# Batch 2's attention numerators in one run, batch 3's k and kv earlier, and PSUM banks placed by hand between batches 0 and 1

## The chip, the cores and the metric

The kernel runs on one core of a Trainium2 chip. The metric is the device time in microseconds (us) of one execution, as the median of several. A profile is one further execution, taken with the hardware profiler; its span runs from the first to the last instruction of the program, and its own device time is a little longer than its span. Engines are named as the profile names them: PE is TensorE's matmuls and PEld its weight loads, DVE is VectorE, ACT is ScalarE, POOL is GpSimd and SP is SyncE, which only issues DMAs here. L533 is line 533 of the kernel before.

## The reference, cut to what matters

Linear attention with the feature map phi, then a token-and-channel mixer, for 8 batches of 8 heads, 576 tokens and 64 columns a head (512 columns in all). All arrays are float32.

```python
phi = lambda x: np.where(x > 0, x, np.exp(x) - 1.0) + 1.0
kv  = einsum('bhsd,bhse->bhde', phi(k), v)
z   = sum(phi(k), axis=2)
num = einsum('bhsd,bhde->bhse', phi(q), kv)
den = einsum('bhsd,bhd->bhs', phi(q), z)[..., None] + 1e-06
x   = (num / den)  # batch, tokens 576, columns 512
h   = relu(x.T @ w_tok1) @ w_tok2          # 576 -> 256 -> 576, along the tokens
u   = x + h.T
out = u + relu(u @ w_ch1) @ w_ch2          # 512 -> 1536 -> 512, along the columns
```

## The kernel before, in words

All matmuls are in bf16 with float32 sums in PSUM, which the kernel holds as one tile of eight banks (128 partitions x 512 float32 each). The 576 tokens of a batch are four slabs of 128 rows (R = 4) and a tail of 64; the tails of two batches share one slab of 128.

For each batch n the steps are, with the names of the code:

- `phi` (L166): exp on ScalarE (`phi_exp`, L148, tile e), x+1 and max on VectorE (`phi_add`, L154, tile y), their minimum on VectorE (`phi_end`, L162, tiles kp and qp). Each is done in two halves c = 0, 1. `prep_k` (L725) is phi of k and the cast of v (`vcast`, L173, tile vs); `k_exp` is only the two exps of a later batch's k.
- `kv` (L181): 72 small matmuls (L188) give kv and z of all heads in two banks; two ScalarE copies (L194) put them into `kvbd`. The first 36 need the first halves of kp and vs, the others the second.
- phi(q) is transposed into qT, by TensorE for batches 0 and 1, by two DMA transposes (`qtr_dma`, L218) from batch 2 on.
- `nd`: numerator and denominator, and the quotient x. In batches 1 and 2 it is six separate steps nd00 to nd21 (L282), each with two or four matmuls of 128 x 130 (L229), and three VectorE instructions (L238, L240, L241). From batch 3 on it is `nd_all` (L249): 40 matmuls of 64 rows x 65 columns (L258) into banks 2 to 7, in three rounds, and eleven VectorE instructions (L267, L269, L271, L278).
- `mm1` (L296): 10 matmuls, two relus on ScalarE (L305, tile ar). `mm2` (L307): ar times w_tok2, and u = x + h.T on VectorE (L327). Batch 1 does this in halves of the columns (`mm2_half`, L342): its first two slabs get x by an identity matmul (L351) and are copied out by ScalarE (L357), its last two by a VectorE addition (L359); `mm2(1, [R])` is batch 1's tail (L315, L323).
- u is transposed to uT: by TensorE in batch 1 (`utr`, L362, transposes L370, evicted by DVE L374 and ACT L376) and for the first tail (`utr_tail`, L508), by DMA transposes (`utr_dma`, L517) from batch 2 on.
- `mm3` (L527): 12 groups (mc) of four matmuls of 512 columns (L533), a relu each (ACT L540, or DVE L537 where dve is set) into cr. `mm3_tail` (L542) does the same for a pair's tails, four mc to a bank.
- `mm4` (L553): 12 accumulating matmuls (L559) to an output slab t, then `mm4_end`: DVE adds u (L576, L586) and GpSimd issues the output's DMA. From batch 3 on the output is made of fewer, other products (L695); their sums of weights are `weight_sums` (L609) on GpSimd.

The order is written out by hand. `run(bigs, fill)` (L877) walks a list of big steps (an mm3 group, an mm3 tail, or four matmuls of mm4) and after big step s it issues all fill steps with the number s. Each engine takes its instructions in the order of the program, and so do the DMA queues of SP and GpSimd. Batch 0's block (L897) ends with twelve steps `m4_0(kc)`, each a matmul for four output slabs; after the last come mm4_end, mm2_half, utr and mm2 of batch 1 (L913). Batch 1's block (L924) has 30 big steps: 12 mm3 groups, three tails, and slabs 4 to 8 of mm4 in three steps each; the numbers in `at1` and the lists under it place batch 2's and batch 3's steps in it.

`bank()` and `banks()` (L65, L70) without a number hand out banks 0 to 3 singly and banks 4 to 7 in pairs, in a ring: a step that is handed a bank waits until its last reader is done. With a number they give that bank. Up to batch 1's block most steps take the ring; from batch 2 on the banks are written out.

Of the kernel before, what the change touches and what calls it, by code (L numbers as in the profile page):

```python
# [18 lines left out]
def kernel(  # L19
# [26 lines left out]
    R = 4  # L46
# [98 lines left out]
    def phi_exp(nm, n, j0, nj):  # L145
        f = raw[nm, rb(n)][:, j0:j0 + nj].rearrange("p j f -> p (j f)")
        e = work.tile([128, 2 * TD], BF16, name="e", tag="e", bufs=4)[:, :nj * TD]
        nc.scalar.activation(out=e, in_=f, func=AF.Exp)  # L148
        live["e", j0] = e
# [8 lines left out]
    def phi_end(nm, n, j0, nj):  # L158
        c, i = divmod(j0, 2)
        dst = (kp if nm == "k" else qp)[:, c, :, i:i + nj]  # L160
        e, y = live["e", j0], live["y", j0][:, :nj * TD]
        live["phi"] = nc.vector.tensor_tensor(  # L162
            out=dst.transpose([0, 2, 1, 3]), in0=e.rearrange("p (i t d) -> p i t d", i=nj, t=T),
            in1=y.rearrange("p (i t d) -> p i t d", i=nj, t=T), op=ALU.min)
# [16 lines left out]
    def kv(n, cs):  # L181
        b = n % 2
        ps = banks(4 if n > 2 else None)[:, :, 0:2 * D1].rearrange(
# [112 lines left out]
    def mm1(n):  # L296
        b = n % 2
        ps = banks(4 if n > 2 else None)
# [8 lines left out]
    def mm2(n, rs, add=False):  # L307
# [4 lines left out]
            None if n < 3 else 4 if rs[0] else 6)  # L312
# [29 lines left out]
    def mm2_half(n, c):  # L342
        b = n % 2
        cs = COLS[c]
        for rs in ([0, 1], [2, 3]):
            ps = banks()[:, 0].rearrange(
# [15 lines left out]
    def utr(n, js):  # L362
        b = n % 2
        for jp in js:
            tp = two16()[:, 0].rearrange(
                "p (j r) c -> p j r c", j=2)
# [5 lines left out]
            dst = uT[b][:, :, 2 * jp:2 * jp + 2].transpose([0, 2, 1, 3])  # L372
            if jp == 0:
                nc.vector.tensor_copy(out=dst, in_=tp)  # L374
            else:
                nc.scalar.copy(out=dst, in_=tp)  # L376

# [147 lines left out]
    def mm3(n, mc, kjs=range(NDM), dve=False):  # L527
        b = n % 2
        if kjs[0] == 0:
            part_of[mc] = bank((0, 1, 0, 1, 2, 3, 0, 1, 2, 3, 0, 1)[mc] if n > 1 else None)  # L530
# [11 lines left out]
    def mm3_tail(i, late=True):  # L542
        ps = bank((2, 3, 0)[i] if late else None).rearrange("p (m s) -> p m s", m=4)
# [9 lines left out]
    def mm4(p, t, kcs, wait=False):  # L553
        if kcs[0] == 0:
            held[t] = bank({0: 2, 1: 3, 2: 0, 3: 2, 8: 3 if p == B // 2 - 1 else 2}[t] if p else None)
# [300 lines left out]
    def steps(n):  # L856

        out_ = [("kv", lambda: kv(n, range(2)))] if n < 3 else []
# [3 lines left out]
        for i, rs in enumerate(([0, 1], [2, 3], [4])) if n < 3 else ():  # L862
            for g in range(2):
                out_.append((f"nd{i}{g}", lambda g=g, rs=rs: nd(n, g, rs)))
        if n > 2:
            out_.append(("nd", lambda: nd_all(n)))
# [21 lines left out]
    m3t_0 = [lambda i=i: mm3_tail(i, False) for i in range(3)]  # L888
# [4 lines left out]
    def m4_0(kc):  # L893
        for t in range(R):
            mm4(0, t, [kc], wait=True)
# [16 lines left out]
    for nm, fn in first[1:2] + late + first[2:3] + first[0:1] + first[3:]:  # L912
# [3 lines left out]
        lambda: mm4_end(0, 2), lambda: mm2_half(1, 1), lambda: utr(1, [0]),  # L916
# [16 lines left out]
    fill += [(27, lambda: weight_sums(0, 2)), (28, lambda: kv(3, range(2)))]
    fill += [(29, lambda: k_exp(4))]
# [92 lines left out]
```

## Time and profile before

| | |
|---|---|
| median of three runs | 256.38 us (256.32 to 256.69) |
| the profiled execution, its own time | 256.18 us |
| its span | 254.3 us |
| batch 0's block and the change to batch 1, up to the first mm3 of batch 1 | to 52.62 us |
| batch 1's block, up to the first mm3 of batch 2 | 52.62 to 86.61 us |
| batches 2 to 7 | 86.61 to 254.3 us |
| DMA engines busy, queues of SP and GpSimd | 46.2% and 22.4% of the span |

The page gives busy times and their share of the span, the granted clock of TensorE in 40 slices, and the chain of work that ended last. A timeline gives instructions of one engine in order of time, merged by line, with the engine's idle time before them and what ended it. The start of a DMA and its landing come from the trace's issues. Instructions of one engine overlap a little: a row's length is the time from start to result, and the next may start before it is over.

### The profile page before, as it was taken

How to read it: one execution, taken by the hardware profiler on the slowest of the kernel's cores; microseconds unless marked ns; L12 is line 12 of the kernel's file. 1: busy time of each engine (PE TensorE's matmuls, PEld its weight loads, DVE VectorE, ACT ScalarE, POOL GpSimd, SP SyncE). 2: the span in 40 equal slices, each digit the busy share in tenths (PEclk: the TensorE clock that was granted, in tenths of full speed). 3: DMA queues.
4: the chain of work that ended last, by engine and by line, in shares of the span. 5: the costliest groups of instructions: out<-in, count | busy, mean ns of one | idle time of the engine just before them, and what ended most of it. 6: DMA issues, size and time to landing. Idle time of an engine off the chain costs nothing.

```text
span 254.3 us, 5671 instructions
## 1 busy us (share of the span) xinstructions
PE 246.2 (97%) x2338; PEld 145.8 (57%) x2338; DVE 162.3 (64%) x288; ACT 138.0 (54%) x217; POOL 68.2 (27%) x84
## 2 busy tenths in 40 slices
PE   7999999989999999999999999999999999999993
PEld 3574455544744444444488545675588545764863
DVE  5965768856767495537955398948864353933543
ACT  4765781559673469515957168565863165127400
POOL 9670120110001763991002600051003500150000
PEclk9999999999999999999999999999999999999999
DMA  6999999999819976459855966669272440445034
GB/s 251 258 203 265 366 233 363 279 261 389 316 42 175 289 261 216 96 131 333 327 125 115 372 148 214 133 176 335 86 116 44 100 110 0 82 61 127 3 92 114
DMA packets 49769, 48.37 MB, mean 190 GB/s; under 512 B 30096, under 2 KB 35600, under 8 KB 49744
## 3 DMA queue, kind: packets, MB, share of 16 engines
q1 hardware_dynamic: 41568, 34.87, 46.2%
q0 software_dynamic: 7632, 12.49, 22.4%
q10 hardware_dynamic: 544, 0.66, 1.1%
q8 instruction: 18, 0.29, 0.5%
q14 instruction: 7, 0.06, 0.1%
HBM read 35.85 MB, written 9.44 MB: 178 GB/s over the span
## 4 chain that ended last, share of the span: by engine, by line
PE 80%; DMA 8%; ACT 4%; POOL 3%; DVE 2%; issue 1%; SPq 0%; POOLq 0%; ACTq 0%; DVEq 0%
PE ps L533 28%; PE ps L695 15%; PE ps L559 14%; PE ps L302 6%; PE ps L547 4%; DMA k_raw<-in_k_dram 4%; PE ps L315 4%; DMA wc<-in_moe_w_ch_dram 4%; PE ps L648 4%; PE ps L188 2%; ACT e L148 2%; PE ps L258 1%; DVE obuf L576 1%; ACT cr L540 1%; PE ps L229 1%
## 5 line engine op out<-in xcount | busy, mean ns | idle before, releaser
L533 PE MATMUL ps<-uT,wc 128*128 128x512 bf16 x384 | 87.2, 379 | 0.8 <-DVE obuf L576 0.4
L540 ACT ACTIVATE cr<-ps 128x512 bf16<-128x512 f32 x91 | 53.1, 600 | 38.9 <-PE ps L533 38.5
L533 PEld LDWEIGHTS <-wc 128*128 128x128 bf16 x384 | 36.9, 98 | 44.3 <-issue 2.2
L559 PE MATMUL ps<-wc,cr 128*128 128x512 bf16 x144 | 34.5, 379 | 0.1
L708 POOL TENSOR_TENSOR obuf<-obuf,q_raw 128x512 f32<-128x512 f32 x4 | 5.1, 1267 | 77.3 <-ACT w L700 58.8
L327 DVE TENSOR_TENSOR u<-ps,x 128x1024 bf16<-128x1024 f32 x12 | 14.7, 1224 | 12.7 <-PE ps L315 12.6
L559 PEld LDWEIGHTS <-cr 128*128 128x128 bf16 x144 | 13.5, 98 | 14.8 <-issue 0.6
L148 ACT ACTIVATE e<-q_raw 128x1152 bf16<-128x1152 f32 x16 | 18.0, 1159 | 7.1 <-DMA q_raw<-in_q_dram 7.1
L630 DVE TENSOR_TENSOR v_raw<-cr 128x768 bf16<-128x768 bf16 (+1 forms) x15 | 10.3, 688 | 15.7 <-ACT cr L540 15.7
L581 POOL DMA_DIRECT2D out_dram<-obuf x12 | 7.3, 613 | 48.1 <-DVE obuf L576 48.1
L148 ACT ACTIVATE e<-k_raw 128x1152 bf16<-128x1152 f32 x16 | 18.2, 1162 | 3.7 <-DMA k_raw<-in_k_dram 3.6
L706 DVE TENSOR_TENSOR obuf<-ps,u 128x512 f32<-128x512 f32 x16 | 11.0, 690 | 12.4 <-PE ps L695 9.5
L695 PE MATMUL ps<-k_raw,v_raw 128*128 128x256 bf16 x144 | 16.7, 273 | 0.0
L695 PEld LDWEIGHTS <-cr 128*128 128x128 bf16 x144 | 14.0, 98 | 2.9
L695 PEld LDWEIGHTS <-v_raw 128*128 128x128 bf16 x144 | 13.9, 98 | 2.8 <-issue 0.8
L271 DVE TENSOR_TENSOR x<-ps,dens 128x768 bf16<-128x768 f32 x15 | 14.4, 958 | 0.5
L194 ACT CAST kvbd<-ps 64x260 bf16<-64x260 f32 x14 | 5.2, 373 | 17.1 <-PE ps L188 17.0
L302 PE MATMUL ps<-x,w 128*128 128x512 bf16 x56 | 14.4, 379 | 0.0
L162 DVE TENSOR_TENSOR kp<-e,y 128x1152 bf16<-128x1152 bf16 x16 | 11.7, 753 | 3.7 <-ACT e L148 3.4
L173 ACT CAST vs<-v_raw 128x1152 bf16<-128x1152 f32 x12 | 13.5, 1161 | 0.0
L154 DVE TENSOR_SCALAR y<-k_raw 128x1152 bf16<-128x1152 f32 x16 | 11.7, 752 | 2.5 <-DMA k_raw<-in_k_dram 2.5
L162 DVE TENSOR_TENSOR qp<-e,y 128x1152 bf16<-128x1152 bf16 x16 | 12.1, 758 | 1.6 <-ACT e L148 0.3
(132 smaller groups left out, 362.8 us busy)
## 6 DMA issues: line engine op xcount, KB each, us to landing
k_raw<-in_k_dram SPq DMA_DIRECT2D x16, 576.0 KB, 7.1
q_raw<-in_q_dram SPq DMA_DIRECT2D x16, 576.0 KB, 6.3
v_raw<-in_v_dram SPq DMA_DIRECT2D x14, 576.0 KB, 10.0
out_dram<-obuf POOLq DMA_DIRECT2D x8, 512.0 KB, 6.7
wc<-in_moe_w_ch_dram POOLq DMA_DIRECT2D x8, 384.0 KB, 10.1
out_dram<-obuf POOLq DMA_DIRECT2D x12, 256.0 KB, 7.3
out_dram<-obuf POOLq DMA_DIRECT2D x6, 128.0 KB, 5.5
cr<-in_v_dram POOLq DMA_DIRECT2D x2, 288.0 KB, 7.5
```

What stands on the lines that cost most here:

```text
L148: nc.scalar.activation(out=e, in_=f, func=AF.Exp)
L154: nc.vector.tensor_scalar(out=y, in0=f, scalar1=1.0, scalar2=1.0, op0=ALU.add, op1=ALU.max)
L162: live["phi"] = nc.vector.tensor_tensor(out=dst.transpose([0, 2, 1, 3]), in0=e.rearrange("p (i t d) -> p i t d", i=nj, t=T), in1=y.rearran ...
L173: copy(out=vs[:, js, :, 0:D], in_=raw["v", rb(n)][:, js].rearrange("p j (t d) -> p j t d", t=T))
L271: nc.vector.tensor_tensor(out=xv[:, :, rc0:rc0 + 3], in0=v_[:, :, k0:k0 + 6, 0:D].rearrange("p i (q a) d -> p i q a d", a=2), in1=den[:, : ...
L302: nc.tensor.matmul(out=ps[:, mt], lhsT=w1t[:, b, ms] if r == R else w1[:, r, ms], rhs=x[b][:, r, :], start=(r == 0), stop=(r == R))
L327: nc.vector.tensor_tensor(out=u[b][:, rs[0]:rs[0] + m], in0=ps[:, 0:m], in1=x[b][:, rs[0]:rs[0] + m], op=ALU.add)
L533: nc.tensor.matmul(out=ps, lhsT=wc1[:, kj, 128 * mc:128 * mc + 128], rhs=uT[b][:, :, kj], start=(kj == 0), stop=(kj == NDM - 1))
L540: nc.scalar.activation(out=cr[b][:, mc, :], in_=ps, func=AF.Relu)
L559: nc.tensor.matmul(out=ps, lhsT=crt[:, kc, :] if t == 8 else cr[b][:, kc, 128 * r:128 * r + 128], rhs=wc2[:, kc, :], start=(kc == 0), stop ...
L695: nc.tensor.matmul(out=live[tile_][:, j], lhsT=lhs[:, k_], rhs=rhs[:, k_], start=(first and j == 0 and k_ == 0), stop=(k_ == KH - 1), skip ...
L706: nc.vector.tensor_tensor(out=o, in0=live[tile_], in1=u[n % 2][:, d::2, HC[c]], op=ALU.add)
```

## The change

Six edits go together:

- `utr` and `mm2_half` of batch 1 take banks 4 to 7 by number, one to each piece (`bank(4 + 2 * c + rs[0] // 2)`, `bank(4 + 2 * jp)`). The two copies of a transposed half are no longer one engine's: ScalarE copies the first 512 columns of the bank and VectorE the second. In the list after `m4_0`, mm4_end(0, 2) comes after the first utr.
- mm3 of batch 1 and its tails take banks from a table, and so do slabs 4 to 8 of mm4 in its block; slabs 0 to 3 of the first pair keep the ring.
- `m4_0` does steps 0 and 1 for slabs 0 and 1 first, then for slabs 2 and 3.
- Batch 2's nd is `nd_all` in one step after big step 10, in place of six steps after 10 to 15; kv, mm1 and mm2 of batch 2 take the fixed banks of later batches, and mm1 and the first mm2 come one step sooner (16 and 18).
- Batch 3's phi(q) comes at 13 and 14 (was 15 and 16), its prep_k at 17 and 21 (24 and 26), weight_sums(0, 2) and k_exp(4) at 22 (27 and 29), kv(3) at 25 (28). So k_exp(4) now stands ahead of kv(3) in the program, and weight_sums ahead of the outputs of slabs 6 to 8.
- The key of the dictionary that holds e takes the name and the batch too.

```diff
@@ -146,7 +146,7 @@
         f = raw[nm, rb(n)][:, j0:j0 + nj].rearrange("p j f -> p (j f)")
         e = work.tile([128, 2 * TD], BF16, name="e", tag="e", bufs=4)[:, :nj * TD]
         nc.scalar.activation(out=e, in_=f, func=AF.Exp)
-        live["e", j0] = e
+        live["e", nm, n, j0] = e
 
     def phi_add(nm, n, j0, nj):
         f = raw[nm, rb(n)][:, j0:j0 + nj].rearrange("p j f -> p (j f)")
@@ -158,7 +158,7 @@
     def phi_end(nm, n, j0, nj):
         c, i = divmod(j0, 2)
         dst = (kp if nm == "k" else qp)[:, c, :, i:i + nj]
-        e, y = live["e", j0], live["y", j0][:, :nj * TD]
+        e, y = live["e", nm, n, j0], live["y", j0][:, :nj * TD]
         live["phi"] = nc.vector.tensor_tensor(
             out=dst.transpose([0, 2, 1, 3]), in0=e.rearrange("p (i t d) -> p i t d", i=nj, t=T),
             in1=y.rearrange("p (i t d) -> p i t d", i=nj, t=T), op=ALU.min)
@@ -180,7 +180,7 @@
 
     def kv(n, cs):
         b = n % 2
-        ps = banks(4 if n > 2 else None)[:, :, 0:2 * D1].rearrange(
+        ps = banks(4 if n > 1 else None)[:, :, 0:2 * D1].rearrange(
             "p a (c e) -> p a c e", c=2)
         for c in cs:
             for t in range(T):
@@ -295,7 +295,7 @@
 
     def mm1(n):
         b = n % 2
-        ps = banks(4 if n > 2 else None)
+        ps = banks(4 if n > 1 else None)
         for mt in range(NT):
             ms = slice(128 * mt, 128 * mt + 128)
             for r in range(R1):
@@ -309,7 +309,7 @@
         b = n % 2
         m = len(rs)
         ps = bank().rearrange("p (a d) -> p a d", a=1) if n == 1 else banks(
-            None if n < 3 else 4 if rs[0] else 6)
+            None if n < 2 else 4 if rs[0] else 6)
         for i, r in enumerate(rs):
             for kt in range(NT):
                 nc.tensor.matmul(out=ps[:, i], lhsT=w2v(kt, r, b),
@@ -343,7 +343,7 @@
         b = n % 2
         cs = COLS[c]
         for rs in ([0, 1], [2, 3]):
-            ps = banks()[:, 0].rearrange(
+            ps = bank(4 + 2 * c + rs[0] // 2).rearrange(
                 "p (r c) -> p r c", r=2)
             add = rs[0] == 0
             for i, r in enumerate(rs):
@@ -362,21 +362,14 @@
     def utr(n, js):
         b = n % 2
         for jp in js:
-            tp = two16()[:, 0].rearrange(
-                "p (j r) c -> p j r c", j=2)
+            tp = bank(4 + 2 * jp).bitcast(BF16).rearrange("p (j r c) -> p j r c", j=2, r=R)
             for i in range(2):
                 j = 2 * jp + i
                 for r in range(R):
                     nc.tensor.transpose(out=tp[:, i, r, :],
                                         in_=u[b][:, r, 128 * j:128 * j + 128], identity=identity)
-            dst = uT[b][:, :, 2 * jp:2 * jp + 2].transpose([0, 2, 1, 3])
-            if jp == 0:
-                nc.vector.tensor_copy(out=dst, in_=tp)
-            else:
-                nc.scalar.copy(out=dst, in_=tp)
-
-
-
+            for i, copy in enumerate((nc.scalar.copy, nc.vector.tensor_copy)):
+                copy(out=uT[b][:, :, 2 * jp + i], in_=tp[:, i])
 
     COLS = [slice(0, DM // 2), slice(DM // 2, DM)]
 
@@ -527,7 +520,9 @@
     def mm3(n, mc, kjs=range(NDM), dve=False):
         b = n % 2
         if kjs[0] == 0:
-            part_of[mc] = bank((0, 1, 0, 1, 2, 3, 0, 1, 2, 3, 0, 1)[mc] if n > 1 else None)
+            part_of[mc] = bank(None if n == 0 else (
+                (0, 1, 0, 1, 2, 3, 0, 1, 2, 3, 0, 1) if n > 1 else
+                (3, 5, 7, 1, 3, 0, 2, 1, 3, 0, 1, 0))[mc])
         ps = part_of[mc]
         for kj in kjs:
             nc.tensor.matmul(out=ps, lhsT=wc1[:, kj, 128 * mc:128 * mc + 128],
@@ -540,7 +535,7 @@
             nc.scalar.activation(out=cr[b][:, mc, :], in_=ps, func=AF.Relu)
 
     def mm3_tail(i, late=True):
-        ps = bank((2, 3, 0)[i] if late else None).rearrange("p (m s) -> p m s", m=4)
+        ps = bank(((2, 3, 0) if late else (1, 2, 3))[i]).rearrange("p (m s) -> p m s", m=4)
         for m in range(4):
             mc = 4 * i + m
             for kj in range(NDM):
@@ -552,7 +547,8 @@
 
     def mm4(p, t, kcs, wait=False):
         if kcs[0] == 0:
-            held[t] = bank({0: 2, 1: 3, 2: 0, 3: 2, 8: 3 if p == B // 2 - 1 else 2}[t] if p else None)
+            held[t] = bank(None if wait else {0: 2, 1: 3, 2: 0, 3: 2, 4: 0, 5: 1, 6: 2, 7: 3,
+                                              8: 3 if p == B // 2 - 1 else 2}[t])
         ps = held[t]
         b, r = divmod(t, R)
         for kc in kcs:
@@ -855,14 +851,14 @@
 
     def steps(n):
 
-        out_ = [("kv", lambda: kv(n, range(2)))] if n < 3 else []
+        out_ = [("kv", lambda: kv(n, range(2)))] if n < 2 else []
         if n == 1:
             puts = [nc.scalar.copy, nc.vector.tensor_copy if n == 1 else nc.scalar.copy]
             out_ += [(f"qt{c}", lambda c=c: qtr(n, c, puts[c])) for c in range(2)]
-        for i, rs in enumerate(([0, 1], [2, 3], [4])) if n < 3 else ():
+        for i, rs in enumerate(([0, 1], [2, 3], [4])) if n < 2 else ():
             for g in range(2):
                 out_.append((f"nd{i}{g}", lambda g=g, rs=rs: nd(n, g, rs)))
-        if n > 2:
+        if n > 1:
             out_.append(("nd", lambda: nd_all(n)))
         out_.append(("mm1", lambda: mm1(n)))
         if n > 1:
@@ -885,14 +881,15 @@
 
     m3 = lambda n, k0=0: [lambda mc=mc: mm3(n, mc) for mc in range(k0, NCH)]
     m3t = [lambda i=i: mm3_tail(i) for i in range(3)]
-    m3t_0 = [lambda i=i: mm3_tail(i, False) for i in range(3)]
     m4 = lambda p, ts: [lambda t=t, i=i: mm4(p, t, range(4 * i, 4 * i + 4))
                         for t in ts for i in range(3)]
 
 
     def m4_0(kc):
-        for t in range(R):
-            mm4(0, t, [kc], wait=True)
+        ts, kcs = (range(2 * kc, 2 * kc + 2), [0, 1]) if kc < 2 else (range(R), [kc])
+        for k_ in kcs:
+            for t in ts:
+                mm4(0, t, [k_], wait=True)
 
     big = [lambda mc=mc: mm3(0, mc, range(2, 4)) for mc in range(3)] + \
         [lambda mc=mc: mm3(0, mc, dve=mc in (3, 6, 9)) for mc in range(3, NCH)] + \
@@ -913,7 +910,7 @@
         fill += [(at0[nm], fn)]
     fill += [(23, fn) for fn in (
         lambda: mm4_end(0, 0), lambda: mm4_end(0, 1), lambda: mm2_half(1, 0),
-        lambda: mm4_end(0, 2), lambda: mm2_half(1, 1), lambda: utr(1, [0]),
+        lambda: mm2_half(1, 1), lambda: utr(1, [0]), lambda: mm4_end(0, 2),
         lambda: mm2(1, [R]), lambda: utr(1, [1]), lambda: mm4_end(0, 3))]
     run(big, sorted(fill, key=lambda e: e[0]))
 
@@ -921,17 +918,17 @@
     for mc in range(3):
         mm3(1, mc, range(0, 2))
     utr_tail(0)
-    big = [lambda mc=mc: mm3(1, mc, range(2, 4)) for mc in range(3)] + [lambda mc=mc: mm3(1, mc, dve=mc in (5, 8)) for mc in range(3, NCH)] + m3t_0 + m4(0, [4, 5, 6, 7, 8])
-    at1 = {"kv": 8, "nd00": 10, "nd01": 11, "nd10": 12, "nd11": 13, "nd20": 14, "nd21": 15,
-           "mm1": 17, "mm2a": 19, "mm2b": 20, "mm2t": 21, "uta": 19, "utb": 20}
+    big = [lambda mc=mc: mm3(1, mc, range(2, 4)) for mc in range(3)] + [lambda mc=mc: mm3(1, mc, dve=mc in (5, 8)) for mc in range(3, NCH)] + [
+        lambda i=i: mm3_tail(i, False) for i in range(3)] + m4(0, [4, 5, 6, 7, 8])
+    at1 = {"nd": 10, "mm1": 16, "mm2a": 18, "mm2b": 20, "uta": 18, "utb": 20}
     fill = [(s, lambda g=g: phi("k", 2, g)) for g, s in ((0, 0), (1, 2))]
     fill += [(4, lambda: vcast(2, 0)), (5, lambda: vcast(2, 1, nc.vector.tensor_copy))]
+    fill += [(8, lambda: kv(2, range(2)))]
     fill += [(at1[nm], fn) for nm, fn in steps(2)]
-    fill += [(s, lambda g=g: phi("q", 3, g)) for g, s in ((0, 15), (1, 16))]
-    fill += [(6, lambda: load_all(4, "k")), (16, lambda: qtr_dma(3)), (23, lambda: load_all(4, "qv"))]
-    fill += [(s, lambda g=g: prep_k(3, g)) for g, s in ((0, 24), (1, 26))]
-    fill += [(27, lambda: weight_sums(0, 2)), (28, lambda: kv(3, range(2)))]
-    fill += [(29, lambda: k_exp(4))]
+    fill += [(s, lambda g=g: phi("q", 3, g)) for g, s in ((0, 13), (1, 14))]
+    fill += [(6, lambda: load_all(4, "k")), (15, lambda: qtr_dma(3)), (22, lambda: load_all(4, "qv"))]
+    fill += [(s, lambda g=g: prep_k(3, g)) for g, s in ((0, 17), (1, 21))]
+    fill += [(22, lambda: k_exp(4)), (22, lambda: weight_sums(0, 2)), (25, lambda: kv(3, range(2)))]
     run(big, sorted(fill, key=lambda e: e[0]))
 
     for n in range(2, B - 1):
```

## The prediction, made before the changed kernel was run

> **What bounds the kernel now.** I read the page's busy times first, then its chain, then the waits, then TensorE's timeline. From the page:
>
> ```profile
> PE 246.2 (97%) x2338; PEld 145.8 (57%) x2338; DVE 162.3 (64%) x288; ACT 138.0 (54%) x217; POOL 68.2 (27%) x84
> PEclk9999999999999999999999999999999999999999
> PE 80%; DMA 8%; ACT 4%; POOL 3%; DVE 2%; issue 1%; SPq 0%; POOLq 0%; ACTq 0%; DVEq 0%
> ```
>
> TensorE is busy 97% of the span at full clock and holds 80% of the chain that ended last. So a microsecond is worth having only where TensorE loses it: by a stall, or by matmuls that could be cheaper. The list of waits shows such stalls only near the places that the change touches (batch 0 to batch 1, and batch 1's block). TensorE's timeline there:
>
> ```profile
> 48.62 0.82 PE L354 MATMUL ps<-ar,w2p 128*128 128x256 bf16 x6
> 49.67 0.27 PE L351 MATMUL ps<-x,identity 128*128 128x256 bf16 x1 [0.24 <-ACT u L357]
> 50.10 0.82 PE L354 MATMUL ps<-ar,w2p 128*128 128x256 bf16 x6
> 51.16 0.61 PE L370 MATMUL ps<-identity,u 128*128 128x128 bf16 x8 [0.24 <-ACT u L357]
> 52.03 0.61 PE L370 MATMUL ps<-identity,u 128*128 128x128 bf16 x8
> 52.62 1.02 PE L533 MATMUL ps<-uT,wc 128*128 128x512 bf16 x4
> 54.06 0.59 PE L533 MATMUL ps<-uT,wc 128*128 128x512 bf16 x2 [0.43 <-DVE obuf L576]
> ```
>
> The columns are start, length, and idle time before. Idle time understates the loss, because a matmul's length is its latency. I take the last start of a group (start + length - one mean) and add one spacing. Spacings come from undisturbed groups: 24 matmuls of 512 columns in 5.34 us at a mean of 379 ns give (5340-379)/23 = 216 ns; likewise 109 ns at 256 columns, 56 at 128. Then the L354 group should hand over at 48.62+0.82-0.27+0.11 = 49.28 and the next starts at 49.67: **0.39 lost**; before 51.16, **0.40**; before 52.62, 0.14; before 54.06 (52.62+1.02-0.38+0.22 = 53.48), **0.58**. Together 1.51 us.
>
> ```profile
> 63.88 0.40 PE L229 MATMUL ps<-kvbd,qT 128*128 128x130 bf16 x4
> 64.12 1.03 PE L533 MATMUL ps<-uT,wc 128*128 128x512 bf16 x4
> ...
> 84.67 0.48 PE L188 MATMUL ps<-vs,kp 64*64 64x65 bf16 x36
> 85.33 0.48 PE L188 MATMUL ps<-vs,kp 64*64 64x65 bf16 x36 [0.17 <-DVE kp L162]
> 85.74 1.04 PE L559 MATMUL ps<-wc,crt 128*128 128x512 bf16 x4
> 86.61 1.89 PE L533 MATMUL ps<-uT,wc 128*128 128x512 bf16 x8
> 88.44 0.79 PE L258 MATMUL ps<-kvbd,qT 64*128 64x65 bf16 x40
> 89.56 2.75 PE L533 MATMUL ps<-uT,wc 128*128 128x512 bf16 x12 [0.33 <-ACT cr L540]
> ```
>
> Here kv(3) stops between its halves (84.67+0.48-0.19+0.01 = 84.97 against 85.33: **0.36**), and after nd(3) TensorE resumes at 89.56 instead of 89.05: 0.51. The same handover one block later costs 0.11 (L258 x40 at 115.73 with the same length, L533 at 116.45), so **0.40** of it is a stall.
>
> **The change part by part.**
>
> *mm2_half and its transposes on banks of their own.* Both 0.4 us stalls are the wait for a ScalarE eviction of u out of a bank that the ring hands out again. Banks 4 to 7 give each piece its own; their last readers (nd and the two relus of mm1, over by 47.25) are done. Both stalls go. The second half runs 49.28 to 50.37 (ten matmuls of 109 ns), the first eight transposes to 50.82, L315 to 51.25, the second eight to 51.70. VectorE's u lands at 50.53+0.69 = 51.22, just ahead of the third of those transposes at 51.36.
>
> *Split eviction of uT.* The row for ScalarE's 128x512 copy (L513) is 590 ns, VectorE's (L501) 425. The first transposes land at 51.0, so ScalarE is done at 51.6. Does VectorE's half run beside it? No row of the trace has both engines reading one bank. [...] In the built program the VectorE copy does wait on ScalarE[...]. The second mm3 matmul (due 51.92) then starts at 52.08: **0.17 lost**. VectorE goes on with obuf t2 to 52.7 and ut to 53.4, so the tail's transposes, due at 53.16, start at 53.47: **0.31 lost**. [...]
>
> *mm3's banks.* The 0.58 stall is mc 2 waiting for a bank that still holds the first block's output tile. In the new table mc 0 to 2 take banks 3, 5, 7 (read out by 49.0, 50.2, 51.3). mc 3 takes the late one; it is due at 54.9, and obuf t3 ends near 54.6. So this stall goes. Boundary: 1.51-0.17-0.31 = **1.03 gained**. A 0.15 wait of mm3 on ScalarE's relus (in the group from 54.72) moves along with both engines and stays.
>
> *m4_0's order.* At 32.09 four L559 matmuls take 1.40 instead of 1.03: 0.37 lost to relus that free banks. The new order avoids it. But kv(1), at 36.29, starts when ScalarE's cast of v (35.03, 1.21) ends, and ScalarE works without a gap from 29.97 to there. The stall moves to kv(1): **0**. The other bound is 0.37.
>
> *nd of batch 2 in one run.* Old: four groups of 0.24 (63.88 to 64.12) and two of 0.12 = 1.20. New, by the rows of nd one block later: 0.72 (115.73 to 116.45), plus 0.09 on entering = 0.81. **0.39 gained**. [...] The row has 15 ns[...]. VectorE: three rounds of 0.17+0.24+0.96 and two of 0.28 are 4.7 us at most, pipelined 4.4. They start near 62.9 and end at 67.3; mm1(2), one step sooner, is due near 69. The first round frees banks 2 and 3 at 64.5, before tail 1 wants bank 2 at 66.7. No new wait.
>
> *Batch 3's k and kv sooner.* kp is ready about 2 us before kv(3) is due, so the **0.36** goes. The two exps of k(4) (2.22 us) now stand in front of kvbd(3), not behind it. Their data landed at 70.5 and they start at 76. kvbd(3) is free of them at 78, kv(3) comes at 80.5. The relus of block 2 then find ScalarE idle: **0.40**. What is pushed back: on VectorE, y and kp (1.5 us) stand ahead of u(2); ScalarE brings their exp at 71.8, so u(2) starts near 74.3, at most 0.4 after its matmuls. On GpSimd, weight_sums (7 us) passes two output DMAs, which nobody waits for. On SP, the transposes of qT(3) and of u(2) keep their order and move 2 us up. The second u(2) transpose took 6.1 us (79.1 to 85.2) for a block that started at 86.61. Now it would be issued near 77.6 and land at 83.7; block 2 wants it at 84.8. Cover: 1.1 us.
>
> **Sum.** 1.03+0.39+0.36+0.40 = 2.18 us. After nd(3) TensorE has no stall above 0.13 us, so the rest moves up whole. The profiled execution took 256.18 (span 254.3 and 1.9 around it), 0.20 below the median of 256.38. The span becomes 252.1, its own time 254.0, the median **254.2**.
>
> **Rivals.**
> 1. *m4_0's stall is a gain too*: if ScalarE follows TensorE there, 0.37 more: 253.8. Against it: ScalarE's gapless row.
> 2. *A transfer takes the place*: the second u(2) transpose lands late. Other such transposes took 3.0 us; this one met two output DMAs issued just before it, and will again. Two microseconds more (8.1) cost 0.9: 255.1.
> 3. *VectorE and ScalarE serialise worse at the boundary*: the stalls turn into waits for uT and ut, gaining nothing there: 255.2.
> 4. *Slower*: batch 3's k is late. Its exp now stands in ScalarE's queue ahead of u(2), through VectorE's kp. It landed at 63.4 and 64.8 and is wanted at 71.8. With 1.5 us of cover behind it, every microsecond after 73.3 delays block 2 by one; slower than before begins at 73.3+2.2+0.5 = 76, 11 us later than it landed. At 77: 257.2.
>
> **How the numbers follow.** Likeliest 254.2: 0.68; rival 1: 0.10; rival 2: 0.09; rival 3: 0.08; rival 4: 0.03; the rest, no change at all, 0.02. The range is 253.5 to 255.2, from a little under rival 1 to rivals 2 and 3. A measurement of this kernel tells about 0.2% (0.5 us) from no change: faster 0.94, same 0.03, slower 0.03.
>
> **What would show it.** In the new timeline: no idle before the second half of mm2_half nor before its transposes; a wait of about 0.2 before the second mm3 of batch 1 and of about 0.3 before the tail's transposes; nd(2) as one group of 40; kv(3) as one group of 72; L533 back 0.11 after nd(3); kv(1) still at 36.3. mm3(2) should start near 84.8. I am wrong if it starts with an idle of its own for the transpose, or if VectorE's x of batch 2 ends after mm1(2) is due.

## The result, and the profile after

| | before | changed |
|---|---|---|
| median (first set, 4 runs each) | 256.53 us (256.32 to 256.79) | 254.00 us (253.94 to 254.60) |
| ratio | | 0.9906 (0.9888 to 0.9925) |
| profiled execution, its own time | 256.18 us | 254.60 us |
| its span | 254.3 us | 252.8 us |

The changed kernel is faster by 0.94% (0.75 to 1.12%), 2.4 us of 256.5; forecast were 254.2 us and 2.2 us. A second measurement of the same kernel gave 253.97 us, ratio 0.9908 (0.9896 to 0.9921).

The page of the changed kernel: TensorE's busy time, and the engines' shares of the chain that ended last.

```profile
PE 244.1 (97%) x2358; PEld 144.6 (57%) x2358; DVE 161.3 (64%) x282; ACT 138.3 (55%) x218; POOL 68.0 (27%) x84
...
PE 90%; DMA 3%; ACT 2%; DVE 2%; issue 1%; SPq 0%; DVEq 0%; ACTq 0%
```

TensorE has 20 matmuls more (nd) and is still busy 2.1 us less. Its timeline between batches 0 and 1 (start, length, line, tiles; line numbers have moved: L528 is mm3, L555 is mm4, L369 the transposes of utr, L504 the tail's transposes, L372 the copies to uT, L572 the output's addition):

```profile
49.14 0.82 PE L354 MATMUL ps<-ar,w2p 128*128 128x256 bf16 x6
49.80 0.27 PE L351 MATMUL ps<-x,identity 128*128 128x256 bf16 x1
...
50.23 0.82 PE L354 MATMUL ps<-ar,w2p 128*128 128x256 bf16 x6
50.89 0.61 PE L369 MATMUL ps<-identity,u 128*128 128x128 bf16 x8
...
52.25 1.62 PE L528 MATMUL ps<-uT,wc 128*128 128x512 bf16 x6
53.96 0.40 PE L504 MATMUL ps<-identity,ut 128*128 128x128 bf16 x4
```

The two 0.4 us stalls are gone: L351 follows L354 after 0.66, six spacings of 109 ns, and so does L369. The 0.58 before the third mm3 group is gone too. What is new is inside the group of six L528 (1.62 long; five spacings of 216 ns and a length of 379 make 1.46, so 0.16 lost) and behind it (52.25+1.62-0.38+0.22 = 53.71 against 53.96: 0.25 lost). Where both come from is in the copies of uT, ScalarE's timeline and then VectorE's:

```profile
51.53 0.59 ACT L372 COPY uT<-ps 128x512 bf16<-128x512 bf16 x1 [0.30 <-PE ps L369]
```

```profile
52.15 0.42 DVE L372 COPY uT<-ps 128x512 bf16<-128x512 bf16 x1 [0.30 <-ACT uT L372]
52.49 0.68 DVE L572 TENSOR_TENSOR obuf<-ps,u 128x512 f32<-128x512 f32 x1
53.20 0.69 DVE L323 TENSOR_TENSOR ut<-ps,x 64x512 bf16<-64x512 f32 x1
```

VectorE stood idle for 0.30 until ScalarE's copy of the other half of the same bank ended (51.53+0.59 = 52.12). The second mm3 matmul had to wait for VectorE's copy (the 0.16), and the tail's transposes for ut, which ended at 53.89, behind slab 2's output (the 0.25).

Batch 1's block and its end, TensorE again:

```profile
63.45 0.79 PE L258 MATMUL ps<-kvbd,qT 64*128 64x65 bf16 x40
64.18 1.04 PE L528 MATMUL ps<-uT,wc 128*128 128x512 bf16 x4
...
81.20 0.89 PE L188 MATMUL ps<-vs,kp 64*64 64x65 bf16 x72
...
85.49 1.89 PE L528 MATMUL ps<-uT,wc 128*128 128x512 bf16 x8
87.32 0.79 PE L258 MATMUL ps<-kvbd,qT 64*128 64x65 bf16 x40
```

nd(2) is one group of 0.73. kv(3) is one group, 0.1 us longer than the kv of other batches (0.89 against 0.78). By the single records of the trace its second half follows the first after 0.02, without a stop; the 0.1 lies near its end, between the starts of the 64th and the 65th of the 72 matmuls. After nd(3) the next mm3 (L528, 88.04) starts 0.72 later, as in the later blocks.

Absolute times are not compared below, because the profiled executions differ by up to 0.65 us ahead of kv(1) (kv(1) starts between 36.16 and 36.81). From the start of mm2_half on they agree to 0.02 us between two profiles of one kernel. So the gains are read from TensorE's starts behind that point (each figure is rounded by itself):

| us between TensorE's starts | before | changed | gain |
|---|---|---|---|
| mm2_half to the tail's transposes | 6.32 | 5.25 | 1.07 |
| tail's transposes to mm1(2); one step of 0.86 fewer lies between | 16.70 | 15.50 | 0.34 |
| mm1(2) to nd(3); one step more | 17.25 | 17.86 | 0.25 |
| nd(3) to mm1(3) | 6.30 | 5.91 | 0.39 |
| mm1(3) to the last matmul | 155.45 | 155.44 | 0.01 |
| mm2_half to the last matmul | 202.01 | 199.97 | 2.04 |

The trace thus explains 2.04 us. The intervals of both measurements (1.9 to 2.9 and 2.0 to 2.7 us) hold it; their middles are 0.3 to 0.4 above. The profiled executions are no typical ones: that of before is 0.35 under its median (256.18 against 256.53), that of the changed kernel 0.60 over its own (254.60 against 254.00).

### The profile page after: what moved, and what is told of

It is laid out like the page before. It is cut to its first block, busy times and chain, and to the rows that moved or that the text cites. A ratio compares the mean times of both kernels' runs of the same rounds, so it can differ in the third digit from the quotient of the medians.

```text
span 252.8 us, 5704 instructions
## 1 busy us (share of the span) xinstructions
PE 244.1 (97%) x2358; PEld 144.6 (57%) x2358; DVE 161.3 (64%) x282; ACT 138.3 (55%) x218; POOL 68.0 (27%) x84
## 4 chain that ended last, share of the span: by engine, by line
PE 90%; DMA 3%; ACT 2%; DVE 2%; issue 1%; SPq 0%; DVEq 0%; ACTq 0%
PE ps L528 33%; PE ps L555 16%; PE ps L691 15%; PE ps L302 6%; PE ps L542 4%; PE ps L315 4%; PE ps L644 4%; DMA q_raw<-in_q_dram 3%; PE ps L188 2%; PE ps L258 2%; PE ps L463 1%; PE ps L473 1%; PE ps L354 1%; PE ps L336 1%; PE ps L229 0%
## 5 line engine op out<-in xcount | busy, mean ns | idle before, releaser
L528 PE MATMUL ps<-uT,wc 128*128 128x512 bf16 x384 | 87.2, 379 | 0.0
L528 PEld LDWEIGHTS <-wc 128*128 128x128 bf16 x384 | 36.8, 98 | 43.5 <-issue 1.5
L555 PE MATMUL ps<-wc,cr 128*128 128x512 bf16 x144 | 34.3, 379 | 0.0
L555 PEld LDWEIGHTS <-cr 128*128 128x128 bf16 x144 | 13.4, 98 | 14.7 <-issue 0.4
L702 DVE TENSOR_TENSOR obuf<-ps,u 128x512 f32<-128x512 f32 x16 | 11.0, 689 | 12.4 <-PE ps L691 9.5
L271 DVE TENSOR_TENSOR x<-ps,dens 128x768 bf16<-128x768 f32 x18 | 17.2, 958 | 0.6
L173 ACT CAST vs<-v_raw 128x1152 bf16<-128x1152 f32 x12 | 13.5, 1162 | 0.0
L572 DVE TENSOR_TENSOR obuf<-ps,u 128x512 f32<-128x512 f32 x12 | 8.2, 688 | 7.9 <-PE ps L555 7.8
L315 PE MATMUL ps<-ar,w2p 128*128 128x512 bf16 x50 | 12.9, 379 | 0.0
```

Of the source, the lines that this page charges most:

```text
L173: copy(out=vs[:, js, :, 0:D], in_=raw["v", rb(n)][:, js].rearrange("p j (t d) -> p j t d", t=T))
L271: nc.vector.tensor_tensor(out=xv[:, :, rc0:rc0 + 3], in0=v_[:, :, k0:k0 + 6, 0:D].rearrange("p i (q a) d -> p i q a d", a=2), in1=den[:, : ...
L315: nc.tensor.matmul(out=ps[:, i], lhsT=w2v(kt, r, b), rhs=ar[b][:, kt, :], start=(kt == 0), stop=(kt == NT - 1 and not add))
L528: nc.tensor.matmul(out=ps, lhsT=wc1[:, kj, 128 * mc:128 * mc + 128], rhs=uT[b][:, :, kj], start=(kj == 0), stop=(kj == NDM - 1))
L555: nc.tensor.matmul(out=ps, lhsT=crt[:, kc, :] if t == 8 else cr[b][:, kc, 128 * r:128 * r + 128], rhs=wc2[:, kc, :], start=(kc == 0), stop ...
L702: nc.vector.tensor_tensor(out=o, in0=live[tile_], in1=u[n % 2][:, d::2, HC[c]], op=ALU.add)
```

## The experiments

All kernels but one start from the changed one. Each ratio is to the kernel before as it was measured in the same set (its median was 256.29 or 256.45), so ratios compare better than medians do. The column on the right is the stretch of the profiled execution from mm2_half to the last matmul, which the noise ahead of kv(1) doesn't touch. Before the change it is 202.01.

| kernel | median us | ratio to before | stretch us |
|---|---|---|---|
| changed kernel, second measurement | 253.97 | 0.9908 (0.9896 to 0.9921) | 199.95 |
| old m4_0 | 254.04 | 0.9911 (0.9899 to 0.9924) | 199.96 |
| boundary alone, on the kernel before | 255.00 | 0.9949 (0.9936 to 0.9962) | 200.94 |
| k of batch 3 late | 254.83 | 0.9948 (0.9936 to 0.9961) | 200.59 |
| k_exp(4) late | 254.06 | 0.9907 (0.9892 to 0.9922) | 199.98 |
| four banks for uT | 253.86 | 0.9903 (0.9890 to 0.9916) | 199.47 |
| four banks, slab 3 ahead of slab 2 | 256.53 | 1.0009 (0.9983 to 1.0036) | 203.71 |
| six nd steps | 258.12 | 1.0055 (1.0036 to 1.0074) | 204.08 |
| whole copies of uT | 254.28 | 0.9913 (0.9899 to 0.9926) | 199.73 |
| ut first | 254.27 | 0.9916 (0.9902 to 0.9929) | 199.90 |
| six nd steps, q of batch 3 late | 254.55 | 0.9924 (0.9912 to 0.9937) | 200.21 |
| four banks, ut first, bank 7 | 253.60 | 0.9887 (0.9873 to 0.9900) | 199.29 |

**The control.** No edit.

> The changed kernel once more, as the control of this set. My sum says 2.2 us under the kernel before (ratio 0.9915); its first measurement gave 2.5 (0.9906). If m4_0's new order is worth nothing, kv(1) starts where ScalarE's cast of v ends, as before, and 2.2 should come out; if it is worth its 0.37, 2.5 to 2.6. The timeline should again show 0.16 lost before the second mm3 of batch 1 and 0.25 before the tail's transposes.

kv(1) starts at 36.27 (before: 36.29), and all stretches of the first profile repeat within 0.02. By the trace the gain is 2.06.

**The old order of m4_0.**

```diff
-        ts, kcs = (range(2 * kc, 2 * kc + 2), [0, 1]) if kc < 2 else (range(R), [kc])
-        for k_ in kcs:
-            for t in ts:
-                mm4(0, t, [k_], wait=True)
+        for t in range(R):
+            mm4(0, t, [kc], wait=True)
```

> The changed kernel with the old order of m4_0. My theory: the 0.37 us stall comes back inside the first L559 group, kv(1) waits that much less for ScalarE's cast, and the time stays that of the changed kernel (254.0, within 0.1). Rival 1: the time rises by 0.37 (254.4).

The time is that of the control, 0.07 apart. TensorE's timeline of the control, around kv(1) (the trace lacks one record of its first group, which has four matmuls):

```profile
32.13 1.03 PE L555 MATMUL ps<-wc,cr 128*128 128x512 bf16 x3
...
35.22 0.67 PE L199 MATMUL ps<-identity,qp 128*128 128x128 bf16 x9
36.27 0.77 PE L188 MATMUL ps<-vs,kp 64*64 64x65 bf16 x72 [0.38 <-ACT vs L173]
```

and with the old order:

```profile
32.34 1.29 PE L555 MATMUL ps<-wc,cr 128*128 128x512 bf16 x4
...
35.70 0.67 PE L199 MATMUL ps<-identity,qp 128*128 128x128 bf16 x9
36.44 0.78 PE L188 MATMUL ps<-vs,kp 64*64 64x65 bf16 x72
```

The stall sits in the first group (1.29 against 1.03) or in front of kv(1) (35.22+0.67-0.22+0.06 = 35.73, and 36.27 is 0.54 later; with the old order 0.23). The end of ScalarE's cast (L173) decides kv(1) in both; the control's cast, and then that of the old order:

```profile
35.01 1.20 ACT L173 CAST vs<-v_raw 128x1152 bf16<-128x1152 f32 x1
```

```profile
35.18 1.21 ACT L173 CAST vs<-v_raw 128x1152 bf16<-128x1152 f32 x1
```

They end at 36.21 and 36.39, and kv(1) starts 0.06 and 0.05 later. So the new order is worth nothing, and rival 1 falls.

**The boundary alone.** The kernel before with the edits to mm2_half, utr, the list behind m4_0 and the banks of mm3, its tails and mm4; m4_0, nd, and batch 3's places stay.

```diff
-            ps = banks()[:, 0].rearrange(
+            ps = bank(4 + 2 * c + rs[0] // 2).rearrange(
...
-            tp = two16()[:, 0].rearrange(
-                "p (j r) c -> p j r c", j=2)
+            tp = bank(4 + 2 * jp).bitcast(BF16).rearrange("p (j r c) -> p j r c", j=2, r=R)
...
-            part_of[mc] = bank((0, 1, 0, 1, 2, 3, 0, 1, 2, 3, 0, 1)[mc] if n > 1 else None)
+            part_of[mc] = bank(None if n == 0 else (
+                (0, 1, 0, 1, 2, 3, 0, 1, 2, 3, 0, 1) if n > 1 else
+                (3, 5, 7, 1, 3, 0, 2, 1, 3, 0, 1, 0))[mc])
```

> The kernel before with the edits between batches 0 and 1 alone (banks of mm2_half and utr, split copies, table of mm3's banks, order of mm4_end), old m4_0, old nd, old places of k and kv. My theory: 1.03 us of the gain, so 1.0 under the kernel before, with the stalls at kv(3) (0.36) and after nd(3) (0.40) still there. Rival 3 (stalls only turn into waits): nothing gained. If the sum of the change lies in m4_0's order instead, less than 0.7.

The stretch is 1.07 shorter than before (202.01 to 200.94), all of it between mm2_half and the tail (5.25 in place of 6.32). The stalls at kv(3) and after nd(3) are as before (0.36 and 0.40). The time gives 1.3 us (1.0 to 1.6). The parts of this edit (the banks of u, mm3's table, the order of mm4_end) were not run apart; that each of the old waits is gone is read from the timeline.

**Batch 3's k late.**

```diff
-    fill += [(6, lambda: load_all(4, "k")), (15, lambda: qtr_dma(3)), (22, lambda: load_all(4, "qv"))]
-    fill += [(s, lambda g=g: prep_k(3, g)) for g, s in ((0, 17), (1, 21))]
-    fill += [(22, lambda: k_exp(4)), (22, lambda: weight_sums(0, 2)), (25, lambda: kv(3, range(2)))]
+    fill += [(6, lambda: load_all(4, "k")), (15, lambda: qtr_dma(3)), (23, lambda: load_all(4, "qv"))]
+    fill += [(s, lambda g=g: prep_k(3, g)) for g, s in ((0, 24), (1, 26))]
+    fill += [(27, lambda: weight_sums(0, 2)), (28, lambda: kv(3, range(2)))]
+    fill += [(29, lambda: k_exp(4))]
```

> The changed kernel with prep_k(3), weight_sums, kv(3) and k_exp(4) back at their old steps (24 to 29). My theory: 0.76 us slower than the changed kernel (0.36 between the halves of kv(3) and 0.40 after nd(3)), 254.8. A rival: only the wait of kv(3) comes back (0.36), because the relus of block 2 have slack.

0.64 us slower by the stretch (0.26 up to nd(3), 0.38 behind it), 0.86 by the medians. Both stalls are back. That is 0.12 under my 0.76, because the changed kernel loses 0.1 elsewhere in kv(3), which this one doesn't.

**Only k_exp(4) late.**

```diff
-    fill += [(22, lambda: k_exp(4)), (22, lambda: weight_sums(0, 2)), (25, lambda: kv(3, range(2)))]
+    fill += [(22, lambda: weight_sums(0, 2)), (25, lambda: kv(3, range(2))), (29, lambda: k_exp(4))]
```

> The changed kernel with only k_exp(4) back behind kv(3), at step 29; prep_k(3) and kv(3) stay early. My theory: kv(3) keeps its gain, but the two exps (2.2 us) run into the first relus of block 2, and 0.3 to 0.4 us come back after nd(3): 254.3 where the changed kernel has 253.97. A rival: with kvbd(3) long done, the exps start sooner and the relus still find ScalarE idle: nothing lost.

My theory fell and the rival holds: nothing is lost. ScalarE's timeline of this kernel, and then that of the kernel with all of batch 3's k late:

```profile
81.86 0.77 ACT L194 CAST kvbd<-ps 64x260 bf16<-64x260 f32 x2 [5.57 <-PE ps L188]
82.65 2.22 ACT L148 ACTIVATE e<-k_raw 128x1152 bf16<-128x1152 f32 x2
86.25 0.60 ACT L535 ACTIVATE cr<-ps 128x512 bf16<-128x512 f32 x1 [1.38 <-PE ps L528]
```

```profile
84.45 0.77 ACT L194 CAST kvbd<-ps 64x260 bf16<-64x260 f32 x2 [8.38 <-PE ps L188]
85.25 2.22 ACT L148 ACTIVATE e<-k_raw 128x1152 bf16<-128x1152 f32 x2
87.49 1.09 ACT L535 ACTIVATE cr<-ps 128x512 bf16<-128x512 f32 x2
```

The exps follow kvbd(3) at once. With kv(3) three steps sooner they end 1.4 us before the first relu of block 2 starts (82.65+2.22 = 84.87, and 86.25); with a late kv(3) they run into it (85.25+2.22 = 87.47, and 87.49). It is kv(3)'s place that gains the 0.4, not that the exps stand ahead of kvbd(3).

**Four banks for uT.** Column block j of uT goes to bank 4 + j; the tail's transposes go to bank 2 and the third mm3 group to bank 4.

```diff
-            tp = bank(4 + 2 * jp).bitcast(BF16).rearrange("p (j r c) -> p j r c", j=2, r=R)
-            for i in range(2):
+            for i, copy in enumerate((nc.scalar.copy, nc.vector.tensor_copy)):
                 j = 2 * jp + i
+                tp = bank(4 + j).bitcast(BF16)[:, 0:128 * R].rearrange("p (r c) -> p r c", r=R)
...
-            for i, copy in enumerate((nc.scalar.copy, nc.vector.tensor_copy)):
-                copy(out=uT[b][:, :, 2 * jp + i], in_=tp[:, i])
+                copy(out=uT[b][:, :, j], in_=tp)
...
-        tp = two16()
+        tp = banks(2).bitcast(BF16).rearrange("p a (t s) -> p a t s", s=128)
...
-                (3, 5, 7, 1, 3, 0, 2, 1, 3, 0, 1, 0))[mc])
+                (3, 5, 4, 1, 3, 0, 2, 1, 3, 0, 1, 0))[mc])
```

> The changed kernel with the four column blocks of uT of batch 1 in four banks (4, 5, 6, 7) instead of two, so that ScalarE's copy and VectorE's copy never read one bank; the tail's transposes go to bank 2 and the third mm3 group to bank 4. If the order of two readers of one bank costs what my sum says, VectorE's copy no longer follows ScalarE's: the 0.16 wait of mm3 goes and the tail's wait falls from 0.25 to below 0.1: 0.3 us faster than the changed kernel. If VectorE was late for another reason, the waits stay and nothing changes.

ScalarE's first copy of uT, and VectorE's:

```profile
51.04 0.59 ACT L371 COPY uT<-ps 128x512 bf16<-128x512 bf16 x1
```

```profile
51.49 0.41 DVE L371 COPY uT<-ps 128x512 bf16<-128x512 bf16 x1
...
52.54 0.69 DVE L323 TENSOR_TENSOR ut<-ps,x 64x512 bf16<-64x512 f32 x1
```

Now the copies overlap (VectorE's starts at 51.49, ScalarE's ends at 51.63), and neither new wait is left: mm2_half to the tail takes 4.86 instead of 5.25. Both kernels write the same parts of uT, so what made VectorE wait (idle for 0.30 in the changed kernel, not at all here) was the bank. Not all of the gain is the turn-taking, though: with four transposes to a bank in place of eight, ScalarE's first copy starts 0.42 after the first transpose (50.62) and not 0.64. The 0.1 us at kv(3) is gone as well. The stretch is 0.48 shorter. The medians show only 0.11 of it. In the profile the span is 0.2 shorter (252.0 against 252.2), so about 0.3 was lost outside the stretch; whether the other executions lost it too isn't shown.

**Four banks, and slab 3's output ahead of slab 2's.** As four banks, and the edit below. This kernel leaves slab 2 of batch 0 out of the output: the buffers are handed out at slab 2, so slab 3, coming first, is added into slab 1's buffer, and the new buffer with slab 2 is never sent.

```diff
-        lambda: mm2_half(1, 1), lambda: utr(1, [0]), lambda: mm4_end(0, 2),
-        lambda: mm2(1, [R]), lambda: utr(1, [1]), lambda: mm4_end(0, 3))]
+        lambda: mm2_half(1, 1), lambda: utr(1, [0]), lambda: mm2(1, [R]),
+        lambda: utr(1, [1]), lambda: mm4_end(0, 3), lambda: mm4_end(0, 2))]
```

> As the kernel with four banks, and ut, the second transposes' copy and slab 3's output go ahead of slab 2's output in VectorE's queue. The tail's wait for ut should be gone altogether: 0.41 us faster than the changed kernel in all (0.16 and 0.25). A rival: ut is bound by its matmuls and not by VectorE's queue; then no more than with four banks.

So its time says nothing of the gain forecast. VectorE waited 3.9 us for slab 1's buffer to be sent, and mm3's fourth group 2.8 us for VectorE. What it shows is the price of a long stall, told at the end.

**Six nd steps.**

```diff
-        for i, rs in enumerate(([0, 1], [2, 3], [4])) if n < 2 else ():
+        for i, rs in enumerate(([0, 1], [2, 3], [4])) if n < 3 else ():
...
-        if n > 1:
+        if n > 2:
             out_.append(("nd", lambda: nd_all(n)))
...
-    at1 = {"nd": 10, "mm1": 16, "mm2a": 18, "mm2b": 20, "uta": 18, "utb": 20}
+    at1 = {"nd00": 10, "nd01": 11, "nd10": 12, "nd11": 13, "nd20": 14, "nd21": 15,
+           "mm1": 17, "mm2a": 19, "mm2b": 20, "uta": 19, "utb": 20}
```

> The changed kernel with batch 2's nd in six steps again (10 to 15, mm1 at 17 and the first mm2 at 19, as before the change). It computes the same. My theory: TensorE needs 0.34 to 0.39 us more for nd and nothing else changes: 254.3. [...] A rival: x comes late for mm1 or banks collide, and more than 1 us is lost.

The rival came: 4.1 us slower than the changed kernel. VectorE's timeline and then TensorE's:

```profile
68.95 0.76 DVE L162 TENSOR_TENSOR qp<-e,y 128x1152 bf16<-128x1152 bf16 x1
...
70.37 0.75 DVE L154 TENSOR_SCALAR y<-q_raw 128x1152 bf16<-128x1152 f32 x1
71.23 0.76 DVE L162 TENSOR_TENSOR qp<-e,y 128x1152 bf16<-128x1152 bf16 x1
...
72.30 0.42 DVE L241 TENSOR_TENSOR x<-ps,den 128x256 bf16<-128x256 f32 x1
```

```profile
72.78 1.02 PE L302 MATMUL ps<-x,w 128*128 128x512 bf16 x4 [2.03 <-DVE x L241]
```

Batch 3's phi(q), at 13 and 14, puts 3.0 us of VectorE work in front of the last x of batch 2 (half of it in front of the last but one), and mm1(2) waits 2.2 us for it (68.86+1.89-0.38+0.22 = 70.59, and 72.78). The rest of the 4.1 is the dearer nd and a fall of TensorE's clock, told at the end. So the edits are not independent: phi(q) of batch 3 can come this early only because nd_all has all its VectorE work at step 10. The early k is not tied to it, as the next kernel shows.

**Six nd steps, with batch 3's q late again.** As six nd steps, and:

```diff
-    fill += [(s, lambda g=g: phi("q", 3, g)) for g, s in ((0, 13), (1, 14))]
-    fill += [(6, lambda: load_all(4, "k")), (15, lambda: qtr_dma(3)), (22, lambda: load_all(4, "qv"))]
+    fill += [(s, lambda g=g: phi("q", 3, g)) for g, s in ((0, 15), (1, 16))]
+    fill += [(6, lambda: load_all(4, "k")), (16, lambda: qtr_dma(3)), (22, lambda: load_all(4, "qv"))]
```

> Six nd steps in the changed kernel as in the last set, but with batch 3's phi(q) back at 15 and 16, behind the last nd step. In the last set VectorE stood at qp of batch 3, waiting for ScalarE's exp, with the last two x behind it. My theory: with that order mended, nd alone costs TensorE 0.34 to 0.39 us more than in one run, and the 2.2 us wait of mm1 with the half clock after it is gone: 254.3 to 254.4. If the waits stay, six nd steps cannot stand with an early kv of batch 3 for another reason.

The wait is gone. From the tail to mm1(2) it takes 16.71 us, as before the change (16.70): nd in one run saves 0.34 on TensorE, near what the rows of later blocks said (0.39). The whole stretch is 0.26 longer than the control's, since here kv(3) is without its 0.1. Batch 3's k and kv stay early in this kernel, and q is late: an early q costs nothing beside nd_all, but no run shows that it gains anything by itself. (Of the wait itself this expectation was wrong: in the kernel before this one VectorE worked without a gap from 68.11 to 72.72, so it was held not by ScalarE's exp but by its own order.)

**Whole copies of uT.**

```diff
-            for i, copy in enumerate((nc.scalar.copy, nc.vector.tensor_copy)):
-                copy(out=uT[b][:, :, 2 * jp + i], in_=tp[:, i])
+            dst = uT[b][:, :, 2 * jp:2 * jp + 2].transpose([0, 2, 1, 3])
+            (nc.scalar.copy if jp else nc.vector.tensor_copy)(out=dst, in_=tp.transpose([0, 1, 2, 3]))
```

> The changed kernel with each transposed bank copied whole by one engine, as before the change (VectorE the first, ScalarE the second). If two readers of one bank have to take turns, the split gains nothing at the first bank: a whole VectorE copy (0.69 us) ends where the two halves in turn end or earlier. My theory: the 0.16 wait of mm3 falls to about 0.05 and the tail's 0.25 goes, because VectorE is no longer held until ScalarE is done: 0.2 to 0.35 us faster than the changed kernel. A rival: the split is needed, and the whole copies bring 0.3 us of waits back, slower than the changed kernel.

One wait of 0.25 in front of mm3 takes the place of 0.16 and 0.25: mm2_half to the tail takes 5.12, 0.13 less than with the split, so the split on one bank loses a little, by the trace. (The other 0.1 of the stretch is that of kv(3), which this profile doesn't have.) The medians can't tell the two kernels apart.

**ut first.**

```diff
-        lambda: mm2_half(1, 1), lambda: utr(1, [0]), lambda: mm4_end(0, 2),
-        lambda: mm2(1, [R]), lambda: utr(1, [1]), lambda: mm4_end(0, 3))]
+        lambda: mm2_half(1, 1), lambda: utr(1, [0]), lambda: mm2(1, [R]),
+        lambda: mm4_end(0, 2), lambda: utr(1, [1]), lambda: mm4_end(0, 3))]
```

> The changed kernel with one exchange in VectorE's queue: ut ahead of slab 2's output. TensorE's order is the same. My theory: the tail's transposes wait for ut alone, which stands behind 0.65 us of slab 2's output; the 0.25 goes and the 0.16 before mm3 stays. A rival: ut is late because of its matmuls, nothing changes.

The tail's 0.25 went, as expected. But the second half's uT copy, now behind both ut and slab 2, came late: mm3 waited 0.26 for it right behind the tail's transposes. Net 0.06 by the stretch; the wait changed its place.

**Four banks, ut first, and bank 7 for the eighth mm3 group.** As four banks, and:

```diff
-        lambda: mm2_half(1, 1), lambda: utr(1, [0]), lambda: mm4_end(0, 2),
-        lambda: mm2(1, [R]), lambda: utr(1, [1]), lambda: mm4_end(0, 3))]
+        lambda: mm2_half(1, 1), lambda: utr(1, [0]), lambda: mm2(1, [R]),
+        lambda: utr(1, [1]), lambda: mm4_end(0, 2), lambda: mm4_end(0, 3))]
...
-                (3, 5, 7, 1, 3, 0, 2, 1, 3, 0, 1, 0))[mc])
+                (3, 5, 4, 1, 3, 0, 2, 7, 3, 0, 1, 0))[mc])
```

> Four banks for uT of batch 1, ut ahead of both late output slabs in VectorE's queue (slab 2 before slab 3), and mm3 group 7 on bank 7 instead of bank 1, so that it does not wait 0.15 us for group 3's relu. Expected: 0.39 from the first two, 0.15 from the third, 0.1 at kv(3) as with four banks alone: 0.5 to 0.65 us less than the changed kernel, 253.4. If kv(2) then waits for ScalarE's cast, only 0.4 to 0.5.

The stretch is 0.66 shorter than the control's: 0.41 from the boundary, 0.16 from mm3's wait for a relu, 0.10 at kv(3). The ratio, 0.9887, is 0.2% under the control's; their intervals overlap a little (0.9896 to 0.9900), so the times alone would not settle it. By the trace this is the fastest of the kernels.

## Why the prediction was right

The time lies 0.2 us from the forecast, and the mechanism was the right one: TensorE sets the pace, and its lost time is what can be won. Part of the closeness is luck: the forecast of 2.2 us lies between the 2.04 of the trace and the 2.4 of the times. By its terms:

| term | predicted | in the trace | shown by |
|---|---|---|---|
| two waits for u's banks and mm3's bank, less the new waits | 1.03 | 1.07 | boundary alone |
| new wait before mm3, new wait of the tail (in the line above) | 0.17, 0.31 | 0.16, 0.25 | four banks: both go |
| m4_0's order | 0 | 0 | old m4_0 |
| nd in one run | 0.39 | 0.34 | six nd steps, q late |
| kv(3) between its halves | 0.36 | 0.36, less a new 0.11 near its end | k late, four banks |
| ScalarE free for block 2's relus | 0.40 | 0.39 | k late, k_exp(4) late |
| sum | 2.18 | 2.05 | |

*Right, for the reason given.* VectorE's copy behind ScalarE's, where the two share a bank, decided the size of the boundary's gain; the prediction took this order from the built program. By the author's estimate, from the lengths of the two copies (VectorE's 0.43 from 51.24 on in place of from 51.6), 0.4 us more would be won without that order (a loss of 0.05 in place of 0.48), and four banks give 0.39. The traces agree in so far as VectorE's first copy waits for ScalarE's on one bank (idle for 0.30 in the changed kernel), and on two banks starts 0.14 before ScalarE's ends (51.49 and 51.63, four banks); what would come of reading one bank at once no run here shows.

*Mis-sized.* The wait between the halves of kv(3) went whole: the second half follows after 0.02. But five profiles, of four kernels, lose 0.1 in front of one of the last ten matmuls of kv(3) (the 63rd to the 71st), with nothing in sight that they wait for; the other kernels with an early kv(3) (four banks, whole copies and four more) don't. The cause stays open. nd's 0.39 rested on a cost of 0.81 for the new form and 1.20 for the old. By the same rows of the changed kernel the new one costs 0.84: TensorE enters it 0.10 late, it takes 0.73, and the mm3 group behind it loses 0.01.

*Wrong in the reason.* For the 0.40 I named the exps of k(4) that "now stand in front of kvbd(3), not behind it". With them behind it again nothing is lost. kv(3), three steps sooner, releases kvbd(3) and all that follows in ScalarE's queue. The number came out all the same, because it was read from the stall itself.

*The signs.* All came in the second profile, with kv(1) at 36.27 (forecast 36.3) and block 2 at 84.93 (forecast near 84.8). In the first, kv(1) started at 36.81, and all behind it as much later, because TensorE was 0.7 us later already at the first L555 (32.79 against 32.13).

*The rivals.* The second transpose of u(2) took 5.6 us (78.25 to 83.85) and block 2 began at 85.49: cover 1.6 instead of the 1.1 of the sum, and no wait. k(3) landed by 64.4, so rival 4 had no ground; its last figure is mis-added (by its own rule a landing at 77 gives 254.2+77-73.3 = 257.9, not 257.2). VectorE's x of batch 2 ended at 68.5, 1.0 before mm1(2) at 69.5; the forecast had 1.7 there, because it let VectorE begin with nd, and it began 0.5 later.

## What to carry to other kernels

When one engine is busy throughout, list its losses as start against start, not as idle time, and ask of each what is late next: m4_0's stall went and gave nothing, because another engine's queue released the same step (kv(1) starts 0.06 after the end of ScalarE's cast in the control). Where the built program lets two engines evict one PSUM bank only in turn, as here (VectorE idle for 0.30), give them two banks before splitting the work: the split on one bank took 5.25 us over the boundary, no split 5.12, two banks 4.86. Moves of steps belong together: in VectorE's queue the early q of batch 3 cost nothing with one form of nd and 4 us with the other.

## What the runs showed of the hardware

In two profiles TensorE's granted clock fell to half during or after an idle time of 2.8 and 2.0 us, and the stall cost more than itself. With six nd steps TensorE stood still for 2.2 us (2.03 by the idle column), and its granted clock was then 0.50. The stretches, with TensorE's busy time and instructions, weight loads, VectorE, ScalarE and GpSimd, the granted clock, and DMA:

```profile
70.00:72.00 2.00, 0.75 (x4) 0.23 (x3) 1.86 (x4) 0.02 (x1) 0.00 (x0) 1.00 0.00 0
72.00:74.00 2.00, 1.22 (x6) 0.54 (x6) 1.92 (x5) 0.00 (x0) 0.00 (x0) 0.94 0.28 72
74.00:76.00 2.00, 2.00 (x6) 0.67 (x5) 0.00 (x0) 0.60 (x1) 0.00 (x0) 0.50 0.72 178
76.00:78.00 2.00, 2.00 (x8) 0.82 (x7) 0.01 (x1) 1.69 (x3) 0.00 (x0) 0.71 0.19 46
```

By the trace the half clock began at 73.76, 1.0 us after the matmuls had resumed (72.78), and lasted 3.41 us; the granted clocks of 0.94, 0.50 and 0.71 make 3.4 too. Matmuls of 512 columns were then 426 ns apart (five spacings from 73.94 to 76.07) instead of 216. That added 1.7 us to the 2.2 of the wait. With the 0.34 of nd, and without the 0.1 at kv(3), this makes the 4.13 by which the stretch is longer than the control's.

The fall was not in every execution. Of the ten of this kernel, seven had a mean clock of 0.993 (3.41 us at half clock in the profile's 256.8 make that) and took 258.0 to 258.6 us; three had 0.997 to 1.000 and took 256.5 to 256.7, about what the wait and nd make by themselves (253.97+2.19+0.34 = 256.5). So the median of 258.12 is that of executions with a mean clock of 0.993, and by the times the fall is worth 1.5 us.

In the kernel with slab 3 ahead of slab 2 an idle time of 2.8 us went with the same:

```profile
54.00:57.00 3.00, 0.80 (x4) 0.29 (x3) 0.17 (x1) 3.00 (x6) 0.00 (x0) 1.00 1.05 250
57.00:59.00 2.00, 1.43 (x4) 0.55 (x4) 1.90 (x4) 0.71 (x1) 1.19 (x2) 0.55 1.03 399
59.00:61.00 2.00, 2.00 (x7) 0.69 (x5) 1.90 (x3) 0.61 (x2) 0.49 (x1) 0.59 1.04 412
```

Here the half clock ran from 57.22 to 60.63 (0.55 and 0.59 in the stretches), 3.41 us as well, and it began 0.35 before the matmuls resumed (57.57), not 1.0 after. Why a stall went with a fall in one execution and with none in the next is not shown: the executions with a mean clock near 1 left no trace.

In the profile of the kernel before, with stalls of up to 0.58 us between batches 0 and 1, the granted clock is 1.00 over 0 to 252.7 us, and so it is in that of the changed kernel, with an idle time of 1.32 us near its start (up to 8.25). One of the six executions with batch 3's k late had a mean clock of 0.992 and took 255.79 us, 0.9 to 1.1 more than the others; it left no trace either.
